# A decode kernel: wo kept in 36 KB rows by head and quarter of d, O placed there by a masked copy, and 36 transposes of h in place of 144

## The chip, the cores and the metric

The kernel runs on one core of one Trainium2 chip. The metric is device time in microseconds (us); the runs of one kernel in one set lie within 0.12% of each other. "Mix" is the last VectorE instruction, which adds the two gated branches; the output stores follow it. Engine names are those of the profile: PE is TensorE, PEld its weight loads, DVE VectorE, ACT ScalarE, POOL GpSimd, SP the queue that issues nearly all DMAs (556.93 of 557.24 MB in before). Times "at 1292.8 us" count from the start of the profiled span.

## The reference

For 8 sequences and one query token, D = 576, H = 32 heads, Sk = 4096 cached positions, Dh = 128, everything in bf16:

```python
q = (x @ wq).reshape(B, 1, H, Dh).transpose(0, 2, 1, 3)
p = softmax(einsum("bhqd,bhkd->bhqk", q, k_cache) * Dh ** -0.5)
a = einsum("bhqk,bhkd->bhqd", p, v_cache).transpose(...).reshape(B, 1, H * Dh) @ wo
b = gelu(layernorm(x) @ w1 + b1) @ w2 + b2            # F = 4608
g = sigmoid((x * gate_w).sum(-1))
return g * a + (1 - g) * b
```

The two caches are 537 MB of the 557 MB that are read.

## The kernel before

Three SBUF slots of 64 KB per partition hold all that streams: first wq, w1, w2, then the K and V tiles (8.4 MB each) of 32 groups of one sequence and 8 heads, then wo. The head of the program computes Q and the MLP. Its hidden rows h are transposed in 144 small matmuls:

```python
for c in range(4):
    for j in range(NJ):                                   # NJ = 36
        o = ht_ps[c][32 * c:32 * c + 32, j * B:(j + 1) * B]
        i = hrow[32 * c:32 * c + B, j::NJ]
        p_hT = op("tensor", lambda e, ...: e.matmul(o, lhsT=i, rhs=ident[32*c:32*c+B, 32*c:32*c+B], ...), ...)
    v_hT.append(op("vector", ... copy of that quarter to hT_sb ...))
```

Groups 0 and 1 are unrolled; groups 2 to 31 are ten turns of a loop of three. Each group multiplies K by q on DVE, sums on PE, takes the softmax, and does P times V on PE (PV), which ACT takes out of PSUM (`evict`). `gather` then adds the diagonal blocks with a selection matmul and `norm` divides. Every third group PE turns three O rows (`turn`, 16 matmuls), DVE takes the result out of PSUM (`stage`), and POOL puts it into OT (`place_o`):

```python
for r in range(WR):                                       # WR = 4
    i = Orow[:, r::WR]
    for h4 in range(4):
        p_tp[k] = op("tensor", ... e.matmul(tp_ps[32*h4:32*h4+32, r*8:(r+1)*8], lhsT=i, rhs=ident[...], ...), ...)
```

In the tail, wo arrives in five loads with 4.6 and 2.3 KB in a row, and three quarters of the output projection is issued before the turn of the last two groups:

```python
WO = ((0, 4, 0, 4), (4, 6, 0, 4), (6, 7, 0, 4), (7, 8, 0, 2), (7, 8, 2, 4))
...
pv(last); evict(last); gather(last); norm(last)
a_proj(range(6), ...)                 # 96 of 128 matmuls: heads of earlier groups
turn(last // GL, False); stage(last // GL); place_o(last // GL)
p_a = a_proj(range(6, WM), ...)       # 32 matmuls
```

Of the kernel before, what the change touches and what calls it, by code (L numbers as in the profile page):

```python
# [37 lines left out]
WM = H // 4  # L38
G0 = 2
GL = 3  # L40
WR = 4
# [149 lines left out]
def bass_gated_mix__mha_block_cached__mixer_channel_mlp__decode_kernel(  # L191
# [40 lines left out]
    wo_sb = view(SL, WO_SLOT * SLOT, [128, WM, WR * D])  # L232
# [41 lines left out]
    ones = sb("ones", [128, 1], F32)  # L274
    acc = sb("acc", [128, GL, HB], F32)
    OTs = sb("OTs", [128, 2, WR, 4], BF16)
# [3 lines left out]
    Orow = sb("Orow", [128, DH], BF16)  # L280
    OT = sb("OT", [128, WM, WR, B], BF16)
# [19 lines left out]
    bank = [nc.alloc_psum_tensor(f"psb{i}", [128, 512], F32) for i in range(8)]  # L301
# [4 lines left out]
    tp_ps = bank[6]  # L306
    y_ps = bank[7]
    up_ps = [bank[4], bank[5], bank[6]]
    ht_ps = bank[0:4]
# [77 lines left out]
    c_Or = memset("gpsimd", Orow[:], 0.0)  # L387

    def own_head(t, inside, outside):

        a = memset("gpsimd", t[:], inside)
        a = op("gpsimd", lambda e: e.affine_select(out=t[:], in_=t[:], compare_op=ALU.is_ge, fill=outside, base=0,
                                                   pattern=[[-PH, HB]], channel_multiplier=1), [a])
        return op("gpsimd", lambda e: e.affine_select(out=t[:], in_=t[:], compare_op=ALU.is_ge, fill=outside,
                                                      base=PH - 1, pattern=[[PH, HB]], channel_multiplier=-1), [a])

    c_ones = memset("gpsimd", ones[:], 1.0)
    c_hneg = own_head(hneg, 0.0, -60000.0)
    c_ps = [memset("vector", bank[i][:, :], 0.0) for i in (0, 1, 4, 5, 6)]
    c_yps = memset("vector", y_ps[:, :], 0.0)  # L400
# [3 lines left out]
        axis=AX.X, op=ALU.add), [c_id])  # L404
    c_Rows = op("vector", lambda e: e.tensor_reduce(
# [102 lines left out]
    v_hT = []  # L508
    for c in range(4):
        for j in range(NJ):  # L510
            o = ht_ps[c][32 * c:32 * c + 32, j * B:(j + 1) * B]
            i = hrow[32 * c:32 * c + B, j::NJ]
            p_hT = op("tensor", lambda e, o=o, i=i, c=c: e.matmul(  # L513
                o, lhsT=i, rhs=ident[32 * c:32 * c + B, 32 * c:32 * c + B], start=True, stop=True),
                [*v_hrow, *a_Q] if c == j == 0 else ())
        v_hT.append(op("vector", lambda e, c=c: e.tensor_copy(
            out=hT_sb[32 * c:32 * c + 32, :, :].rearrange("p j b -> p (j b)"),
            in_=ht_ps[c][32 * c:32 * c + 32, 0:NJ * B]), [p_hT]))
# [9 lines left out]
    for jt in range(NJ):  # L528
# [9 lines left out]
    a_qb, v_mult, v_red, p_sum, v_nm, a_exp, p_pv, a_ev, p_z, p_oz, v_norm, p_tp, v_st, g_ot, g_qm, p_q = (  # L538
        {} for _ in range(16))
    tp_of = bass.AP(tensor=tp_ps, offset=0, ap=[[pstride(tp_ps), 128], [4, 2], [8, WR], [1, 4]])  # L540

    def q_of(g):
# [5 lines left out]
            [*a_Q, c_sel32, a_ev[g - 3] if looped else p_q.get(g - 1)], token="tensor" if looped else None)  # L548
# [77 lines left out]
    def gather(g):  # L626
        looped = in_loop(g + 2)
        p_z[g] = op("tensor", lambda e: e.matmul(  # L628
            oz_ps[0:HB, DH:DH + 1], lhsT=acc[:, place(g), :], rhs=ones[:, :], start=True, stop=True),
            [a_ev[g], v_norm.get(g - 1), c_ones, *v_hb])  # L630
        for tt in range(TQ):
            p_oz[g] = op("tensor", lambda e, tt=tt: e.matmul(  # L632
                oz_ps[0:HB, 0:DH], lhsT=sel32[:, :, tt], rhs=O_sb[:, tt, :], start=(tt == 0), stop=(tt == TQ - 1)),
                [c_sel32] if tt == 0 else (), token="vector" if looped and tt == TQ - 1 else None)
# [60 lines left out]
    for g in range(NG):  # L695
# [4 lines left out]
        def between(c, g=g, k=k):  # L700
            if c == 1:
                q_of(g + 1)
            if in_loop(g) and place(g) == 0:
                if c == 2:
                    turn(k, True)
                if c == 4:
                    stage(k)
# [85 lines left out]
```

## Time and profile before

| | before |
|---|---|
| time, median of 3 runs | 1297.93 us (1297.68 to 1298.09) |
| span profiled | 1296.3 us |
| busy share PE / DVE / ACT / POOL | 56 / 62 / 12 / 3% |
| DMA, mean of 16 engines | 430 GB/s, 99.5% by the SP queue |
| last wo landing, mix | 1292.8 us, 1293.18 us |

The page of the kernel before: busy us by engine, then the DMA share and the GB/s in 40 slices of the span, then two of the DMA queues with packets, MB and share of 16 engines' span:

```profile
PE 731.7 (56%) x5202; PEld 339.4 (26%) x5202; DVE 804.7 (62%) x833; ACT 160.9 (12%) x587; POOL 40.7 (3%) x82
...
DMA  9999999999999999999999999999999999999997
GB/s 394 436 433 433 434 433 432 433 431 439 433 433 433 431 439 433 433 433 431 439 429 437 433 431 439 429 437 433 431 437 431 437 433 429 439 431 435 435 429 331
...
q1 hardware_dynamic: 11200, 556.93, 99.5%
q8 instruction: 10, 0.16, 0.1%
```

DMA is full from the first slice to the last but one. PE, DVE, ACT and POOL never bound the middle; only the last slice, at 331 GB/s, has something to give.

Two of the costliest groups of before (line, engine, operation, output<-inputs, shapes, count | busy us, mean ns | idle before, and what ended it):

```profile
L561 DVE TENSOR_TENSOR SL<-SL,q_bc 128x4096 bf16<-128x4096 bf16 x256 | 581.4, 2281 | 329.6 <-DMA SL<-in_A_k_cache_dram 329.6
...
L513 PE MATMUL psb<-ident,SL 8*32 8x8 bf16 x144 | 8.0, 196 | 6.6 <-DVE SL L504 6.6
```

DVE stands idle 329.6 us, about 10 us per group, for K to land. The 144 transposes cost PE 8.0 us.

The end of the chain of waits of before (start, us, what):

```profile
1268.56 24.22 DMA SL<-in_A_wo_dram
...
1292.83 0.33 PE psb L523 x8
...
1293.18 0.37 DVE out_sb L753
```

and what the engines did meanwhile, from its timeline:

```profile
1280.34 5.16 PE L617 MATMUL psb<-SL,P 128*32 128x512 bf16 x64 [2.81 <-DMA SL<-in_A_v_cache_dram]
...
1287.04 1.27 PE L523 MATMUL psb<-SL,OT 128*8 128x144 bf16 x58
...
1290.02 0.67 PE L523 MATMUL psb<-SL,OT 128*8 128x144 bf16 x32 [1.71 <-DMA SL<-in_A_wo_dram]
...
1291.13 0.34 POOL L662 COPY OT<-OTs 128x8 bf16<-128x8 bf16 x2 [19.27 <-DVE OTs L657]
...
1291.62 0.81 PE L523 MATMUL psb<-SL,OT 128*8 128x144 bf16 x24 [0.82 <-POOL OT L662]
```

The chain ends on the last wo load, with eight matmuls (0.33 us) behind it. The compute path (last V, PV, gather, turn, POOL's copy, 24 matmuls) is finished at 1291.62 + 0.81 = 1292.43 us, and then waits 0.4 us for wo. It had waited for wo before: the 32 matmuls at 1290.02 us, behind which the turn comes, stood 1.71 us for the second load.

The DMA view of before, of 1289 to 1292.5 us in 40 slices of 0.09 us, shows how the stream drains:

```profile
GB/s 316 448 290 342 290 369 237 290 316 316 211 290 184 211 132 158 105 132 79 79 26 26 53 53 240 26 26 26 26 26 26 26 26 26 26 26 26 26 0 0
```

433 GB/s, the rate of the middle slices, over 16 engines is 27 GB/s for one (an estimate). The run of 26 is one engine alone, finishing its wo rows for over a microsecond after the others are done (the single 240 is a 16 KB packet of queue 8, whose kind the page gives as "instruction"; such a packet is called a fetch below).

### The profile page before, as it was taken

To read this page: it belongs to the slowest core of one execution; us is meant where nothing else is said; L and a number is where in the kernel's file an instruction comes from. 1 tells how busy PE (TensorE), PEld (TensorE's weight loads), DVE (VectorE), ACT (ScalarE), POOL (GpSimd) and SP (SyncE) were. 2 spreads that over 40 slices of the span, in tenths; PEclk is the share of its full clock that TensorE was granted. 3 is DMA by queue.
4 is the path that set the end of the run, shared out by engine and by line. 5 is a ranking of instruction groups with operands and counts; after the bars stand their busy time and mean duration, and the time that the engine had idled before them with its cause. 6 is when DMAs were issued, how large, how long until landed. Compare 5 with 4: busy or idle time off the path is not lost.

```text
span 1296.3 us, 12332 instructions
## 1 busy us (share of the span) xinstructions
PE 731.7 (56%) x5202; PEld 339.4 (26%) x5202; DVE 804.7 (62%) x833; ACT 160.9 (12%) x587; POOL 40.7 (3%) x82
## 2 busy tenths in 40 slices
PE   3577566555566555556555556545556655546655
PEld 1423223122222222223222223222222222223213
DVE  2387667655567665567765567765567765566761
ACT  1011110111110011110011111011111011111011
POOL 1000000000000000000000000000000000000000
PEclk8588898787898778888877898887799878789878
DMA  9999999999999999999999999999999999999997
GB/s 394 436 433 433 434 433 432 433 431 439 433 433 433 431 439 433 433 433 431 439 429 437 433 431 439 429 437 433 431 437 431 437 433 429 439 431 435 435 429 331
DMA packets 11406, 557.24 MB, mean 430 GB/s; under 512 B 1360, under 2 KB 1376, under 8 KB 2816
## 3 DMA queue, kind: packets, MB, share of 16 engines
q1 hardware_dynamic: 11200, 556.93, 99.5%
q8 instruction: 10, 0.16, 0.1%
q10 hardware_dynamic: 192, 0.11, 0.0%
q14 instruction: 4, 0.03, 0.0%
HBM read 557.03 MB, written 0.01 MB: 430 GB/s over the span
## 4 chain that ended last, share of the span: by engine, by line
DMA 56%; DVE 25%; PE 13%; ACT 5%; issue 1%; SPq 0%; ACTq 0%
DMA SL<-in_A_k_cache_dram 53%; DVE SL L561 20%; PE psb L566 7%; DVE s_sb L572 5%; ACT P L606 4%; PE psb L617 4%; DMA SL<-in_A_wo_dram 2%; DMA SL<-in_A_wq_dram 1%; PE psb L632 1%; ACT O_sb L623 1%; PE psb L472 0%; SPq L317 0%; PE psb L628 0%; DVE OTs L657 0%; DVE mA L591 0%
## 5 line engine op out<-in xcount | busy, mean ns | idle before, releaser
L566 PE MATMUL psb<-SL,ident 128*128 128x512 bf16 x2048 | 550.1, 421 | 519.4 <-DVE SL L561 518.9
L561 DVE TENSOR_TENSOR SL<-SL,q_bc 128x4096 bf16<-128x4096 bf16 x256 | 581.4, 2281 | 329.6 <-DMA SL<-in_A_k_cache_dram 329.6
L566 PEld LDWEIGHTS psb<-SL,ident 128*128 128x128 bf16 x2048 | 199.7, 106 | 852.8 <-DVE SL L561 612.1
L572 DVE TENSOR_REDUCE s_sb<-psb 128x32 f32<-128x512 f32 x256 | 175.0, 684 | 91.0 <-PE psb L566 91.0
L606 ACT ACTIVATE P<-s_sb,hb 128x256 bf16<-128x256 f32 x256 | 126.3, 494 | 660.8 <-PE psb L617 643.9
L617 PE MATMUL psb<-SL,P 128*32 128x512 bf16 x2048 | 127.0, 386 | 2.8 <-DMA SL<-in_A_v_cache_dram 2.8
L617 PEld LDWEIGHTS psb<-SL,P 128*32 128x32 bf16 x2048 | 95.8, 153 | 20.4 <-DMA SL<-in_A_v_cache_dram 3.3
L545 POOL TENSOR_SCALAR Qm<-Q,sel 128x256 bf16<-128x256 bf16 x33 | 32.6, 987 | 1030.7 <-ACT O_sb L623 967.1
L553 ACT ACTIVATE q_bc<-psb 128x128 bf16<-128x128 f32 x33 | 9.1, 277 | 420.2 <-PE psb L550 420.2
L606 ACT ACTIVATION_READ_ACCUMULATOR P<-s_sb,hb 128x1 f32 x256 | 47.7, 186 | 0.0
L632 PE MATMUL psb<-O_sb,sel 128*8 128x128 f32 x256 | 33.9, 276 | 0.0
L632 PEld LDWEIGHTS psb<-O_sb,sel 128*8 128x8 f32 x256 | 21.8, 93 | 3.0
L623 ACT ACTIVATE O_sb<-psb 128x512 f32<-128x512 f32 x32 | 18.4, 574 | 10.0 <-PE psb L617 10.0
L638 DVE RECIPROCAL rz<-psb 8x1 f32<-8x1 f32 x32 | 4.8, 149 | 15.5 <-PE psb L632 15.5
L591 DVE TENSOR_REDUCE mA<-s_sb 128x1 f32<-128x256 f32 x32 | 13.4, 420 | 1.1
L494 DVE TENSOR_TENSOR SL<-psb,SL 104x384 f32<-104x384 f32 x3 | 1.7, 552 | 18.7 <-PE psb L490 18.7
L662 POOL COPY OT<-OTs 128x8 bf16<-128x8 bf16 x32 | 5.1, 218 | 219.1 <-DVE OTs L657 219.1
L640 DVE TENSOR_SCALAR Orow<-psb,rz 8x128 bf16<-8x128 f32 x32 | 10.9, 341 | 1.3 <-DVE rz L638 0.2
L513 PE MATMUL psb<-ident,SL 8*32 8x8 bf16 x144 | 8.0, 196 | 6.6 <-DVE SL L504 6.6
L490 PE MATMUL psb<-SL 128*8 128x384 bf16 x60 | 5.8, 519 | 7.1 <-DMA SL<-in_B_w_dram 7.1
L513 PEld LDWEIGHTS psb<-ident,SL 8*32 8x32 bf16 x144 | 7.9, 148 | 7.3 <-DVE SL L504 7.3
L628 PE MATMUL psb<-ones,acc 128*8 128x1 f32 x64 | 6.3, 167 | 5.3 <-ACT O_sb L623 5.3
(71 smaller groups left out, 111.6 us busy)
## 6 DMA issues: line engine op xcount, KB each, us to landing
SL<-in_B_w_dram SPq DMA_DIRECT2D x1, 5184.0 KB, 38.7
SL<-in_B_w_dram SPq DMA_DIRECT2D x1, 4608.0 KB, 25.0
SL<-in_A_wq_dram SPq DMA_DIRECT2D x1, 4096.0 KB, 13.6
SL<-in_A_wo_dram SPq DMA_DIRECT2D x1, 2304.0 KB, 19.4
SL<-in_A_wo_dram SPq DMA_DIRECT2D x1, 1152.0 KB, 23.0
SL<-in_B_w_dram SPq DMA_DIRECT2D x1, 576.0 KB, 26.0
SL<-in_A_wo_dram SPq DMA_DIRECT2D x1, 576.0 KB, 23.8
SL<-in_A_wo_dram SPq DMA_DIRECT2D x2, 288.0 KB, 24.1
```

The costliest lines, as they stand in the source:

```text
L513: p_hT = op("tensor", lambda e, o=o, i=i, c=c: e.matmul(o, lhsT=i, rhs=ident[32 * c:32 * c + B, 32 * c:32 * c + B], start=True, stop=True) ...
L545: g_qm[g] = op("gpsimd", lambda e: e.tensor_scalar(out=Qm[:, :, :].rearrange("p k d -> p (k d)"), in0=Q4[:, 2 * hg * DH:(2 * hg + 2) * DH] ...
L553: a_qb[g] = op("scalar", lambda e: e.activation(out=q_bc[:, place(g), :], in_=qb_ps[:, 0:DH], func=ACT.Copy), [p_q[g]], token="vector" if ...
L561: v_mult[g, c] = op("vector", lambda e: e.tensor_tensor(out=part, in0=part, in1=qb, op=ALU.mult), [land["k", g], a_qb[g]], token="tensor" ...
L566: p_sum[g, c] = op("tensor", lambda e, r=r, n=n: e.matmul(tr_ps[par][:, :], lhsT=ident[:, :], rhs=r, start=(n == 0), stop=(n == NCH - 1)), ...
L572: v_red[g, c] = op("vector", lambda e: e.tensor_reduce(out=s_sb[:, c * CT:(c + 1) * CT], in_=tr_ps[par][:, :].rearrange("p (t c) -> p t c" ...
L591: t = op("vector", lambda e: e.tensor_reduce(out=mA[:, 0:1], in_=s_sb[:, :], axis=AX.X, op=ALU.max), [v_red[g, NCK - 1], c_mA], token=own)
L606: a_exp[g] = op("scalar", lambda e, h=h: e.activation(out=P[:, h, :], in_=s_sb[:, :], func=ACT.Exp, bias=hb8[:, h:h + 1], scale=1.0, accum ...
L617: p_pv[g] = op("tensor", lambda e, o=o, tq=tq: e.matmul(o, lhsT=P[:, :, :].rearrange("p h t -> p (h t)")[:, tq::NTQ], rhs=vb[:, tq::NTQ, : ...
L623: a_ev[g] = op("scalar", lambda e: e.activation(out=O_sb[:].rearrange("p t d -> p (t d)"), in_=o_ps[:, :], func=ACT.Copy), [p_pv[g], p_z.g ...
L632: p_oz[g] = op("tensor", lambda e, tt=tt: e.matmul(oz_ps[0:HB, 0:DH], lhsT=sel32[:, :, tt], rhs=O_sb[:, tt, :], start=(tt == 0), stop=(tt ...
L640: v_norm[g] = op("vector", lambda e: e.tensor_scalar(out=Orow[32 * (g % GL):32 * (g % GL) + HB, :], in0=oz_ps[0:HB, 0:DH], scalar1=rz[0:HB ...
```

## The change

The intent: take work off PE. wo is laid out by 128 rows of 32 x 576 values, row p = (head, quarter of d), so each partition holds 36 KB contiguous in memory. O goes there without a turn: the gather repeats each head over four partitions (`selq`), DVE keeps on each the quarter that belongs to it (mask `dqm`) and folds, and POOL copies once per three groups into the 32 partitions of OT. The 144 transposes of h become 36 with all four quarters at once. PSUM becomes one tensor, cleared by one memset.

```diff
-    for c in range(4):
-        for j in range(NJ):
-            ... 144 matmuls, rhs = 8x8 identity
+    per_quarter = bass.AP(tensor=ident, offset=0, ap=[[pstride(ident), QP], [32, 4], [1, B]])
+    for j in range(NJ):
+        p_hT = op("tensor", lambda e, j=j: e.matmul(
+            ht_ps[0:32, j, :, :], lhsT=hrow[0:QP, j::NJ], rhs=per_quarter, start=True, stop=True), ...)
 ...
     def norm(g):
-        reciprocal; tensor_scalar -> Orow
+        t = tensor_reduce(zs <- oz_ps[0:32, DH:DH + HB]);  t = reciprocal(rz <- zs)
+        t = scalar_tensor_tensor(On <- oz_ps[0:32, 0:DH] * rz * dqm)
+        v_norm[g] = tensor_reduce(OTs[:, :, place(g + 2)] <- On by quarter)
-    def turn(k, looped): ... 16 matmuls
-    def stage(k): ...
+    def place_o(engine, g0, g1): ... OT[32 * hg:32 * hg + 32, :, b:b + n] <- OTs
 ...
-    WO = ((0, 4, 0, 4), (4, 6, 0, 4), (6, 7, 0, 4), (7, 8, 0, 2), (7, 8, 2, 4))
+    WO = ((0, 24), (24, 30), (30, 32))
 ...
-    a_proj(range(6), ...); turn(...); stage(...); place_o(...); p_a = a_proj(range(6, WM), ...)
+    place_o("vector", last - 1, last + 1)
+    for j in range(NJO):                                   # NJO = 32: all 128 matmuls after O
+        p_a = quarters(OT[:, j, :], wo_sb[:, j, :], j == 0, j == NJO - 1, [ld_wo[j], v_bx, *g_ot.values()])
```

More of the change, by code (lines that the diff above doesn't have):

```diff
@@ L37 @@
 FB = FC // 3
-WM = H // 4
+NDQ = 4
+NJO = H * DH // 128
 G0 = 2
 GL = 3
-WR = 4
 class Stream:
@@ L231, in bass_gated_mix__mha_block_cached__mixer_channel_mlp__decode_kernel @@
     WO_SLOT = (2 * NG + 3) % 3
-    wo_sb = view(SL, WO_SLOT * SLOT, [128, WM, WR * D])
+    wo_sb = view(SL, WO_SLOT * SLOT, [128, NJO, D])
     class Tail:
@@ L273, in bass_gated_mix__mha_block_cached__mixer_channel_mlp__decode_kernel @@
     Sel = sb("Sel", [128, 64], BF16)
-    ones = sb("ones", [128, 1], F32)
+    hsel = sb("hsel", [128, HB * NDQ], F32)
+    selq = sb("selq", [128, TQ, HB * NDQ], F32)
+    zs = sb("zs", [32, 1], F32)
     acc = sb("acc", [128, GL, HB], F32)
-    OTs = sb("OTs", [128, 2, WR, 4], BF16)
+    OTs = sb("OTs", [32, NJO, GL], F32)
+    On = sb("On", [32, DH], F32)
+    dqm = sb("dqm", [32, NDQ], F32)
     Rows = sb("Rows", [128, 4], F32)
@@ L279, in bass_gated_mix__mha_block_cached__mixer_channel_mlp__decode_kernel @@
     q_bc = sb("q_bc", [128, GL, DH], BF16)
-    Orow = sb("Orow", [128, DH], BF16)
-    OT = sb("OT", [128, WM, WR, B], BF16)
+    OT = sb("OT", [128, NJO, B], BF16)
     bmg_sb = sb("bmg_sb", [128, QN], F32)
@@ L298, in bass_gated_mix__mha_block_cached__mixer_channel_mlp__decode_kernel @@
     rz = sb("rz", [128, 1], F32)
-    bank = [nc.alloc_psum_tensor(f"psb{i}", [128, 512], F32) for i in range(8)]
+    PS = nc.alloc_psum_tensor("PS", [128, 8 * 512], F32)
+    bank = [PS[:, 512 * i:512 * (i + 1)] for i in range(8)]
     tr_ps = bank[0:2]
@@ L305, in bass_gated_mix__mha_block_cached__mixer_channel_mlp__decode_kernel @@
     oz_ps = bank[5]
-    tp_ps = bank[6]
     y_ps = bank[7]
     up_ps = [bank[4], bank[5], bank[6]]
-    ht_ps = bank[0:4]
+    ht_ps = PS[:, 0:NJ * 32].rearrange("p (j c b) -> p j c b", j=NJ, c=4)
     xt_ps = bank[7]
@@ L386, in bass_gated_mix__mha_block_cached__mixer_channel_mlp__decode_kernel @@
     c_mA = memset("gpsimd", mA[:], 0.0)
-    c_Or = memset("gpsimd", Orow[:], 0.0)
-    def own_head(t, inside, outside):
-        a = memset("gpsimd", t[:], inside)
-        a = op("gpsimd", lambda e: e.affine_select(out=t[:], in_=t[:], compare_op=ALU.is_ge, fill=outside, base=0,
-                                                   pattern=[[-PH, HB]], channel_multiplier=1), [a])
-        return op("gpsimd", lambda e: e.affine_select(out=t[:], in_=t[:], compare_op=ALU.is_ge, fill=outside,
-                                                      base=PH - 1, pattern=[[PH, HB]], channel_multiplier=-1), [a])
-    c_ones = memset("gpsimd", ones[:], 1.0)
-    c_hneg = own_head(hneg, 0.0, -60000.0)
-    c_ps = [memset("vector", bank[i][:, :], 0.0) for i in (0, 1, 4, 5, 6)]
-    c_yps = memset("vector", y_ps[:, :], 0.0)
+    c_ones = memset("gpsimd", hsel[:], 1.0)
+    per_head = hsel[:].rearrange("p (h q) -> p h q", q=NDQ)
+    t = op("gpsimd", lambda e: e.affine_select(out=per_head, in_=per_head, compare_op=ALU.is_ge, fill=0.0, base=0,
+                                               pattern=[[-PH, HB], [0, NDQ]], channel_multiplier=1), [c_ones])
+    c_hsel = op("gpsimd", lambda e: e.affine_select(out=per_head, in_=per_head, compare_op=ALU.is_ge, fill=0.0,
+                                                    base=PH - 1, pattern=[[PH, HB], [0, NDQ]], channel_multiplier=-1), [t])
+    c_hneg = op("vector", lambda e: e.tensor_scalar(out=hneg[:, :], in0=hsel[:, ::NDQ], scalar1=-1.0, scalar2=60000.0,
+                                                    op0=ALU.add, op1=ALU.mult), [c_hsel])
+    c_yps = memset("vector", PS[:, :], 0.0)
+    c_ps = [c_yps]
+    c_dqm = op("vector", lambda e: e.tensor_reduce(
+        out=dqm[:], in_=bass.AP(tensor=ident, offset=0, ap=[[pstride(ident), 32], [1, NDQ], [NDQ, 8]]),
+        axis=AX.X, op=ALU.add), [c_id])
     c_sel32 = op("vector", lambda e: e.tensor_reduce(
@@ L404, in bass_gated_mix__mha_block_cached__mixer_channel_mlp__decode_kernel @@
         axis=AX.X, op=ALU.add), [c_id])
+    c_selq = op("vector", lambda e: e.tensor_copy(
+        out=selq[:].rearrange("p t (h q) -> p t h q", q=NDQ),
+        in_=bass.AP(tensor=sel32, offset=0, ap=[[pstride(sel32), 128], [1, TQ], [TQ, HB], [0, NDQ]])), [c_sel32])
     c_Rows = op("vector", lambda e: e.tensor_reduce(
@@ L506, in bass_gated_mix__mha_block_cached__mixer_channel_mlp__decode_kernel @@
     free[1] = [p_up]
-    v_hT = []
-    for c in range(4):
-        for j in range(NJ):
-            o = ht_ps[c][32 * c:32 * c + 32, j * B:(j + 1) * B]
-            i = hrow[32 * c:32 * c + B, j::NJ]
-            p_hT = op("tensor", lambda e, o=o, i=i, c=c: e.matmul(
-                o, lhsT=i, rhs=ident[32 * c:32 * c + B, 32 * c:32 * c + B], start=True, stop=True),
-                [*v_hrow, *a_Q] if c == j == 0 else ())
-        v_hT.append(op("vector", lambda e, c=c: e.tensor_copy(
-            out=hT_sb[32 * c:32 * c + 32, :, :].rearrange("p j b -> p (j b)"),
-            in_=ht_ps[c][32 * c:32 * c + 32, 0:NJ * B]), [p_hT]))
+    per_quarter = bass.AP(tensor=ident, offset=0, ap=[[pstride(ident), QP], [32, 4], [1, B]])
+    for j in range(NJ):
+        p_hT = op("tensor", lambda e, j=j: e.matmul(
+            ht_ps[0:32, j, :, :], lhsT=hrow[0:QP, j::NJ], rhs=per_quarter, start=True, stop=True),
+            [*v_hrow, *a_Q] if j == 0 else ())
+    v_hT = [op("vector", lambda e, c=c: e.tensor_copy(
+        out=hT_sb[32 * c:32 * c + 32, :, :], in_=ht_ps[0:32, :, c, :]), [p_hT]) for c in range(4)]
     def quarters(lhsT, w, first, stop, waits):
@@ L535, in bass_gated_mix__mha_block_cached__mixer_channel_mlp__decode_kernel @@
     free[2] = [p_down]
-    a_qb, v_mult, v_red, p_sum, v_nm, a_exp, p_pv, a_ev, p_z, p_oz, v_norm, p_tp, v_st, g_ot, g_qm, p_q = (
-        {} for _ in range(16))
-    tp_of = bass.AP(tensor=tp_ps, offset=0, ap=[[pstride(tp_ps), 128], [4, 2], [8, WR], [1, 4]])
+    a_qb, v_mult, v_red, p_sum, v_nm, a_exp, p_pv, a_ev, p_z, p_oz, v_norm, g_ot, g_qm, p_q = ({} for _ in range(14))
     def q_of(g):
@@ L547, in q_of @@
             scalar1=sel32[:, b // TQ, b % TQ:b % TQ + 1], scalar2=None, op0=ALU.mult),
-            [*a_Q, c_sel32, a_ev[g - 3] if looped else p_q.get(g - 1)], token="tensor" if looped else None)
+            [*a_Q, c_sel32, a_ev[g - 3] if looped else p_q.get(g - 1), *list(g_ot.values())[-1:]], token="tensor" if looped else None)
         for k in range(2):
@@ L628, in gather @@
         p_z[g] = op("tensor", lambda e: e.matmul(
-            oz_ps[0:HB, DH:DH + 1], lhsT=acc[:, place(g), :], rhs=ones[:, :], start=True, stop=True),
-            [a_ev[g], v_norm.get(g - 1), c_ones, *v_hb])
+            oz_ps[0:32, DH:DH + HB], lhsT=hsel[:, :], rhs=acc[:, place(g), :], start=True, stop=True),
+            [a_ev[g], v_norm.get(g - 1), c_hsel, *v_hb])
         for tt in range(TQ):
             p_oz[g] = op("tensor", lambda e, tt=tt: e.matmul(
-                oz_ps[0:HB, 0:DH], lhsT=sel32[:, :, tt], rhs=O_sb[:, tt, :], start=(tt == 0), stop=(tt == TQ - 1)),
-                [c_sel32] if tt == 0 else (), token="vector" if looped and tt == TQ - 1 else None)
+                oz_ps[0:32, 0:DH], lhsT=selq[:, tt, :], rhs=O_sb[:, tt, :], start=(tt == 0),
+                stop=(tt == TQ - 1)), [c_selq] if tt == 0 else (),
+                token="vector" if looped and tt == TQ - 1 else None)
@@ L636, in norm @@
     def norm(g):
-        looped = in_loop(g + 2)
-        t = op("vector", lambda e: e.reciprocal(out=rz[0:HB, :], in_=oz_ps[0:HB, DH:DH + 1]), [p_oz[g]],
-               token="vector" if looped else None)
-        v_norm[g] = op("vector", lambda e: e.tensor_scalar(
-            out=Orow[32 * (g % GL):32 * (g % GL) + HB, :], in0=oz_ps[0:HB, 0:DH], scalar1=rz[0:HB, 0:1], scalar2=None,
-            op0=ALU.mult), [t, c_Or, p_tp.get(g // GL - 1) if not looped else None])
-    def turn(k, looped):
-        for r in range(WR):
-            i = Orow[:, r::WR]
-            for h4 in range(4):
-                p_tp[k] = op("tensor", lambda e, r=r, h4=h4, i=i: e.matmul(
-                    tp_ps[32 * h4:32 * h4 + 32, r * 8:(r + 1) * 8], lhsT=i,
-                    rhs=bass.AP(tensor=ident, offset=h4, ap=[[pstride(ident), 128], [4, 2], [32, 4]]),
-                    start=True, stop=True),
-                    [v_norm.get(min(GL * k + GL, NG) - 1), v_st.get(k - 1), *v_hb] if r == h4 == 0 else (),
-                    token="vector" if looped and r == WR - 1 and h4 == 3 else None)
@@ L656, in stage @@
-    def stage(k):
-        v_st[k] = op("vector", lambda e: e.tensor_copy(out=OTs[:, :, :, :], in_=tp_of), [p_tp[k], g_ot.get(k - 1)])
-    def place_o(k):
-        for g in range(GL * k, min(GL * k + GL, NG)):
+        own = "vector" if in_loop(g + 2) else None
+        t = op("vector", lambda e: e.tensor_reduce(out=zs[:, :], in_=oz_ps[0:32, DH:DH + HB], axis=AX.X, op=ALU.add),
+               [p_oz[g]], token=own)
+        t = op("vector", lambda e: e.reciprocal(out=rz[0:32, :], in_=zs[:, :]), [t], token=own)
@@ new lines, in norm @@
+        t = op("vector", lambda e: e.scalar_tensor_tensor(
+            out=On[:, :].rearrange("p (q j) -> p q j", q=NDQ), in0=oz_ps[0:32, 0:DH].rearrange("p (q j) -> p q j", q=NDQ),
+            scalar=rz[0:32, 0:1], in1=bass.AP(tensor=dqm, offset=0, ap=[[pstride(dqm), 32], [1, NDQ], [0, NJO]]),
+            op0=ALU.mult, op1=ALU.mult), [t, c_dqm], token=own)
+        v_norm[g] = op("vector", lambda e: e.tensor_reduce(
+            out=OTs[:, :, place(g + 2)], in_=On[:, :].rearrange("p (q j) -> p j q", q=NDQ), axis=AX.X, op=ALU.add),
+            [t, *list(g_ot.values())[-1:]])
@@ L661, in place_o @@
+    def place_o(engine, g0, g1):
+        g, t = g0, None
+        while g < g1:
             hg, b = divmod(g, B)
-            g_ot[k] = op("gpsimd", lambda e, hg=hg, b=b, g=g: e.tensor_copy(
-                out=OT[:, 2 * hg:2 * hg + 2, :, b], in_=OTs[:, :, :, g % GL]), [v_st[k]])
+            n = min(g1 - g, B - b)
+            t = g_ot[g0] = op(engine, lambda e, hg=hg, b=b, n=n, at=g - g0: e.tensor_copy(
+                out=OT[32 * hg:32 * hg + 32, :, b:b + n], in_=OTs[:, :, at:at + n]), [v_norm[g1 - 1], t])
+            g += n
@@ L681, in bass_gated_mix__mha_block_cached__mixer_channel_mlp__decode_kernel @@
     next_load()
-    WO = ((0, 4, 0, 4), (4, 6, 0, 4), (6, 7, 0, 4), (7, 8, 0, 2), (7, 8, 2, 4))
+    WO = ((0, 24), (24, 30), (30, 32))
     ld_wo = {}
     def load_wo(waits):
-        for n, (m0, m1, r0, r1) in enumerate(WO):
-            src = bass.AP(tensor=A_wo.tensor, offset=A_wo.offset + m0 * 512 * D + r0 * D,
-                          ap=[[WR * D, 128], [512 * D, m1 - m0], [1, (r1 - r0) * D]])
-            t = load("sync", wo_sb[:, m0:m1, r0 * D:r1 * D], src, f"ld_wo{n}", waits)
-            for m in range(m0, m1):
-                for r in range(r0, r1):
-                    ld_wo[m, r] = t
+        w = A_wo.rearrange("(p j) n -> p j n", j=NJO)
+        for n, (j0, j1) in enumerate(WO):
+            t = load("sync", wo_sb[:, j0:j1, :], w[:, j0:j1, :], f"ld_wo{n}", waits)
+            ld_wo.update({j: t for j in range(j0, j1)})
     for g in range(NG):
@@ L697, in bass_gated_mix__mha_block_cached__mixer_channel_mlp__decode_kernel, with between @@
             S.mark()
-        k = (g - G0) // GL - 1
-        def between(c, g=g, k=k):
+        def between(c, g=g):
             if c == 1:
                 q_of(g + 1)
-            if in_loop(g) and place(g) == 0:
-                if c == 2:
-                    turn(k, True)
-                if c == 4:
-                    stage(k)
         scores(g, between)
         if in_loop(g):
-            if place(g) == 0 and k >= 0:
-                place_o(k)
             gather(g - 2)
@@ L723, in bass_gated_mix__mha_block_cached__mixer_channel_mlp__decode_kernel @@
             norm(g - 2)
+            if place(g) == GL - 1:
+                place_o("gpsimd", g - GL - 1, g - 1)
         exps(g)
@@ L730, in bass_gated_mix__mha_block_cached__mixer_channel_mlp__decode_kernel @@
     last = NG - 1
-    turn(last // GL - 1, False)
-    stage(last // GL - 1)
-    place_o(last // GL - 1)
     gather(last - 1)
@@ L739, in bass_gated_mix__mha_block_cached__mixer_channel_mlp__decode_kernel @@
     norm(last)
-    def a_proj(ms, turned):
-        for m in ms:
-            for r in range(WR):
-                at = quarters(OT[:, m, r, :], wo_sb[:, m, r * D:(r + 1) * D], m == r == 0, m == WM - 1 and r == WR - 1,
-                              [ld_wo[m, r], v_bx, *turned])
-        return at
-    a_proj(range(6), list(g_ot.values()))
-    turn(last // GL, False)
-    stage(last // GL)
-    place_o(last // GL)
-    p_a = a_proj(range(6, WM), list(g_ot.values()))
+    place_o("vector", last - 1, last + 1)
+    for j in range(NJO):
+        p_a = quarters(OT[:, j, :], wo_sb[:, j, :], j == 0, j == NJO - 1,
+                       [ld_wo[j], v_bx, *g_ot.values()])
     t = op("vector", lambda e: e.scalar_tensor_tensor(
```

## The prediction

> **What bounds the kernel now.** The DMA stream. In the 40 slices the DMA row is at 9 tenths or more in 39, at a mean of 430 GB/s over 557 MB; queue 1 alone fills 99.5% of 16 engines' span. [...] PE (56%), DVE (62%), ACT (12%), POOL (3%) are under it: DVE idles 329.6 us for K loads (costliest groups). The queue is never empty: K loads take 43.4 us, V loads 33.1 us from issue to landing, where one needs 19.5 us.
>
> **What changes, and what lies on the path.**
> 1. Head. The 144 transposes of h (8.0 us, their copies mostly hidden; timeline, 40.6 to 49.2 us) become 36, an estimated 2 us, then four copies of 0.46 us: w2's slot comes free 4 to 5 us before 55.3 us. V's load into it is issued sooner, but queues behind two K loads, the first landing only at 60.8 us. Gain: 0. One memset of all 8 PSUM banks (6 took 3.19 us, so about 4.3), now behind a POOL mask, delays the LayerNorm chain about 4 us, into the wait for wq (PE idles 4.0 us before 15.99 us); Q may slip a few tenths. K's load is issued at 21 us into a queue full until 39 us. Cost: 0.
> 2. Loop. 16 turns per three groups leave PE; DVE gets four small instructions (estimated 0.9 us) for two (0.49 us), per group of 39 us. All in idle time. Cost: 0.
> 3. Tail, the only place where compute matters. Now the last wo chunk lands at 1292.8 us (chain of waits: 24.2 us of DMA), then 8 matmuls (0.33 us), mix (0.37 us), stores, to 1296.3 us. PE's last turn, POOL's copy (1290.5 to 1291.6 us) and 24 matmuls end at 1292.4 us, 0.4 us before the DMA: the removed turn is almost, not quite, on the path. The wo packets grow from 4.6 and 2.3 KB (1152) to 27.6, 6.9 and 2.3 KB (384). While wo streamed, 1280 to 1288 us, the rate was 407 to 412 GB/s instead of 433: 5% of 11 us, so its end should come 0.5 us sooner. The drain is ragged: from 1289.5 to 1292.5 us DMA share falls from 0.74 to 0.05, a few engines finishing late; larger packets may shorten it. New: O is ready at about 1288.7 us, but 96 of 128 matmuls wait for one load of three quarters of wo, due about 1289.7 us; 128 at 21 ns are 2.7 us, so PE ends about 1292.4 us, together with the last load. Gain: 0.5 us.
>
> **Prediction.** 1297.4 us, 8 in 10 within 1296.2 to 1298.6. Chance of faster by over 2%: 0.005; within 2%: 0.99; slower: 0.005.
>
> **What would show it.** Right: middle slices unchanged at 430 to 433 GB/s; the first K landing at 60.8 us; bmg done 4 to 5 us earlier with nothing later moving; a chain of waits ending wo DMA, few matmuls, mix; the mix at 1292.6 us instead of 1293.2. Wrong: another rate in the loop; a later first K; PE last in the chain by more than 1 us.
>
> **What would make it wrong.** A TensorE clock of 0.5 (as at 1273 to 1283 us) during the last 128 matmuls, 2.5 us; POOL copies or a late q delaying DVE beyond its 10 us of slack; the ragged drain coming from wo's small packets, 1 to 2 us more gain.

The sum is 0 for the head, 0 for the loop and 0.5 us for the tail, so 1297.4 us from the 1297.93 us of before. Estimates from the trace of before are the 19.5 us for one load (8.4 MB at 430 GB/s), the 21 ns for a matmul (32 in 0.67 us) and the 0.5 us itself (5% of 11 us), which supposes that larger packets bring back the whole of the lower rate.

## The result, and the profile after

The changed kernel takes 1296.80 us (median of 6, 1296.61 to 1297.22) against 1297.85 us (median of 6, 1297.65 to 1298.09) of before: 1.05 us less. Ratios are the mean time of one kernel's fast runs over that of the other's of the same rounds, so not quite the ratio of these medians; here 0.9993 with a 95% interval of 0.998 to 1.0005. By that interval the kernels are the same; but all six runs of the changed kernel lie under all six of before, and a second set on another chip gives 1297.00 (1296.71 to 1297.23, 5 runs) against 1297.91 us. About one microsecond, 0.08%, is there.

The page after:

```profile
PE 720.0 (56%) x4902; PEld 333.8 (26%) x4902; DVE 821.5 (63%) x884; ACT 160.9 (12%) x587; POOL 41.0 (3%) x60
...
GB/s 395 437 428 440 430 436 430 433 435 433 433 431 435 437 429 433 433 435 437 425 437 435 433 431 431 437 435 431 435 429 437 435 427 435 435 435 431 429 439 343
...
q1 hardware_dynamic: 10400, 556.93, 99.5%
q8 instruction: 9, 0.15, 0.0%
```

PE lost 11.7 us of work and 300 matmuls, DVE gained 16.8 us, and the slices between the first and the last move the same GB/s, slice by slice within a few per cent. The SP queue moves the same bytes in 800 fewer packets; queue 8 has 9 packets instead of 10.

The end of the chain of waits after:

```profile
1236.94 43.38 DMA SL<-in_A_v_cache_dram
...
1280.36 6.04 PE PS L617 x34
...
1286.43 0.61 ACT O_sb L623
...
1287.31 0.91 PE PS L632 x8
...
1289.38 0.20 DVE OT L656
...
1289.72 2.20 PE PS L525 x128
...
1291.94 0.37 DVE out_sb L727
```

The chain has changed its kind. It no longer ends on wo but runs through compute from the last V landing: PV, eviction, gather, norm, all 128 projection matmuls without a wait. The mix is 1.24 us sooner; the last V load is not (first PV matmul at 1280.36 us, before 1280.34). The last wo load lands 23.8 us after its issue at 1267.5 us, at 1291.3 us instead of 1292.8.

The drain after, in the same window of the DMA view:

```profile
GB/s 184 342 158 237 316 184 290 316 211 211 211 132 53 79 79 79 53 26 26 26 26 0 0 0 0 0 0 0 0 0 0 0 0 0 0 0 187 0 0 0
```

The lone engine at 26 GB/s is left for four slices, 0.35 us, where before it was there for well over one microsecond.

So two questions: what brought wo's landing 1.5 us forward (the prediction had 0.5), and what is the removed turn worth?

### The profile page after: what moved, and what is told of

It reads as the page before. It is cut to its first block, busy times and chain, and to the rows that moved or that the text cites. A ratio compares the mean times of both kernels' runs of the same rounds, so it can differ in the third digit from the quotient of the medians.

```text
span 1295.0 us, 11764 instructions
## 1 busy us (share of the span) xinstructions
PE 720.0 (56%) x4902; PEld 333.8 (26%) x4902; DVE 821.5 (63%) x884; ACT 160.9 (12%) x587; POOL 41.0 (3%) x60
## 4 chain that ended last, share of the span: by engine, by line
DMA 57%; DVE 23%; PE 13%; ACT 5%; issue 1%; ACTq 0%; SPq 0%
DMA SL<-in_A_k_cache_dram 53%; DVE SL L561 19%; PE PS L566 7%; PE PS L617 5%; ACT P L606 4%; DVE s_sb L572 4%; DMA SL<-in_A_v_cache_dram 3%; DMA SL<-in_A_wq_dram 1%; PE PS L632 1%; ACT O_sb L623 1%; PE PS L478 0%; PE PS L628 0%; PE PS L525 0%; SPq L320 0%; DVE OTs L646 0%
## 5 line engine op out<-in xcount | busy, mean ns | idle before, releaser
L566 PE MATMUL PS<-SL,ident 128*128 128x512 bf16 x2048 | 546.9, 419 | 530.3 <-DVE SL L561 530.3
L566 PEld LDWEIGHTS PS<-SL,ident 128*128 128x128 bf16 x2048 | 198.9, 106 | 865.3 <-DVE SL L561 627.4
L572 DVE TENSOR_REDUCE s_sb<-PS 128x32 f32<-128x512 f32 x256 | 175.1, 684 | 89.9 <-PE PS L566 89.7
L617 PE MATMUL PS<-SL,P 128*32 128x512 bf16 x2048 | 127.9, 387 | 2.7 <-DMA SL<-in_A_v_cache_dram 2.7
L617 PEld LDWEIGHTS PS<-SL,P 128*32 128x32 bf16 x2048 | 95.8, 152 | 21.1 <-DMA SL<-in_A_v_cache_dram 3.1
L632 PE MATMUL PS<-O_sb,selq 128*32 128x128 f32 x256 | 34.1, 278 | 0.0
L632 PEld LDWEIGHTS PS<-O_sb,selq 128*32 128x32 f32 x256 | 26.1, 113 | 0.2
L623 ACT ACTIVATE O_sb<-PS 128x512 f32<-128x512 f32 x32 | 18.4, 575 | 10.8 <-PE PS L617 10.8
L646 DVE TENSOR_REDUCE OTs<-On 32x32 f32<-32x128 f32 x32 | 11.9, 371 | 1.1
L642 DVE SCALAR_TENSOR_TENSOR On<-PS,rz,dqm 32x128 f32<-32x128 f32 x32 | 10.8, 339 | 1.2
L500 DVE TENSOR_TENSOR SL<-PS,SL 104x384 f32<-104x384 f32 x3 | 1.7, 552 | 15.3 <-PE PS L496 15.3
```

Source lines behind the costliest of these rows:

```text
L566: p_sum[g, c] = op("tensor", lambda e, r=r, n=n: e.matmul(tr_ps[par][:, :], lhsT=ident[:, :], rhs=r, start=(n == 0), stop=(n == NCH - 1)), ...
L572: v_red[g, c] = op("vector", lambda e: e.tensor_reduce(out=s_sb[:, c * CT:(c + 1) * CT], in_=tr_ps[par][:, :].rearrange("p (t c) -> p t c" ...
L617: p_pv[g] = op("tensor", lambda e, o=o, tq=tq: e.matmul(o, lhsT=P[:, :, :].rearrange("p h t -> p (h t)")[:, tq::NTQ], rhs=vb[:, tq::NTQ, : ...
L623: a_ev[g] = op("scalar", lambda e: e.activation(out=O_sb[:].rearrange("p t d -> p (t d)"), in_=o_ps[:, :], func=ACT.Copy), [p_pv[g], p_z.g ...
L632: p_oz[g] = op("tensor", lambda e, tt=tt: e.matmul(oz_ps[0:32, 0:DH], lhsT=selq[:, tt, :], rhs=O_sb[:, tt, :], start=(tt == 0), stop=(tt = ...
L642: t = op("vector", lambda e: e.scalar_tensor_tensor(out=On[:, :].rearrange("p (q j) -> p q j", q=NDQ), in0=oz_ps[0:32, 0:DH].rearrange("p ...
```

## The experiments

Twelve kernels; names with b are made from the kernel before, with a from the changed one. The interval of every ratio is about plus or minus 0.0014, or 1.8 us. So medians and their ranges, on one chip, are read together with what the trace shows, and differences of 0.2 us are not argued from. The kernel before took 1297.76 us (1297.60 to 1298.38), 1297.64 (1297.46 to 1297.86) and 1297.91 (1297.45 to 1298.31), 9 runs each.

| run | median us (range of 5) | ratio to before | last wo landing, us | mix, us |
|---|---|---|---|---|
| b_wo75 | 1296.59 (1296.24 to 1296.79) | 0.9989 | cut | 1292.05 |
| a_wo75 | 1296.86 (1295.91 to 1297.06) | 0.9990 | cut | 1292.58 |
| a_small | 1297.24 (1296.88 to 1297.92) | 0.9996 | 1291.6 | 1292.04 |
| b_wo3 | 1298.03 (1297.62 to 1299.06) | 1.0000 | 1292.4 | 1294.08 |
| b_h36 | 1297.15 (1297.05 to 1297.34) | 0.9996 | 1291.8 | 1292.18 |
| a_norm3 | 1296.59 (1296.56 to 1297.11) | 0.9993 | 1291.4 | 1291.82 |
| a_vh | 1298.17 (1297.56 to 1298.73) | 1.0004 | 1291.9 | 1293.22 |
| b_vh | 1298.24 (1297.84 to 1298.51) | 1.0004 | 1293.3 | 1293.79 |
| b_h36_pad | 1297.77 (1297.74 to 1298.21) | 1.0000 | 1292.4 | 1292.77 |
| a_pad | 1296.96 (1296.60 to 1297.58) | 0.9994 | 1291.3 | 1292.14 |
| a_ztail | 1297.70 (1296.71 to 1298.05) | 0.9996 | 1291.4 | 1291.83 |
| a_again | 1297.00 (1296.71 to 1297.23) | 0.9993 | 1291.4 | 1292.41 |

Landings are the last issue plus its time to landing. The mix is that of the one profiled run, so it is not always the median run (b_wo3's was its slowest). The profile of before (landing 1292.8, mix 1293.18 us) is of a run of 1298.07 us, 0.1 to 0.4 us above its medians, so differences of landing or mix to it are on the large side.

### What ended the kernel before, and what ends it now: b_wo75 and a_wo75

```diff
 # b_wo75: the last three of five loads left out
-    WO = ((0, 4, 0, 4), (4, 6, 0, 4), (6, 7, 0, 4), (7, 8, 0, 2), (7, 8, 2, 4))
+    WO = ((0, 4, 0, 4), (4, 6, 0, 4))
 # a_wo75: the last two of three loads left out
-    WO = ((0, 24), (24, 30), (30, 32))
+    WO = ((0, 24),)
```

Both leave out the last quarter of wo's bytes and compute a wrong result. (The comparison with the reference evidently does not resolve this part of the output.)

> The kernel before without its last three wo loads (25% of wo; wrong result on purpose, the matmuls read what the K slot held). Theory: before ended on the last wo landing (1292.8 us); without it the turn of the last two groups and POOL's copy end last, mix at about 1292.45 us instead of 1293.18: 0.7 us faster, about 1297.1 us. Rival (before was already limited by its compute path): no change, 1297.85 us.

> The changed kernel without its last two wo loads (25% of wo; wrong result on purpose). Theory: the changed kernel ends on compute after the last V landing, so no change: 1296.8 us, mix still at about 1291.9 us. Rival (it still ends on wo): faster by 0.3 us or more. The difference of this run to the same cut of before is what the removed turn is worth by itself: theory 0.3 to 0.6 us.

Without the last quarter, before is faster by 1.17 us, all five runs below all nine of before on that chip. That is more than the 0.7 us expected: the turn came sooner too (the last 32 matmuls began at 1291.32 us, where the last 32 of before began at 1291.62), as the second wo load, for which it waits, landed 0.2 us sooner. The changed kernel does not move (1296.86 against 1296.80 and 1297.00 elsewhere). So before ended on wo and the changed kernel does not; that much is shown. The ends of their chains of waits, b_wo75 first:

```profile
1291.14 0.13 POOL OT L662
...
1291.32 0.70 PE psb L523 x32
...
1292.05 0.37 DVE out_sb L753
```

```profile
1290.02 0.20 DVE OT L656
...
1290.36 2.20 PE PS L525 x128
...
1292.58 0.37 DVE out_sb L727
```

Their difference is what the new compute path is worth by itself, with wo out of the way. I expected 0.3 to 0.6 us for the changed kernel; the runs give 0.27 us to before, which is to say nothing measurable. In before the turn and POOL's copy come after 96 of the 128 matmuls, and only 32 (0.70 us) follow O. In the changed kernel O needs no turn, but all 128 (2.20 us) follow it. From the start of PV (1280.41 and 1280.43 us) to the mix it is 11.64 us in the one and 12.15 in the other, of which 0.35 us is a longer PV in a_wo75 (6.59 against 6.24 us, at a granted clock of 0.65 from 1280 to 1289 us where b_wo75 has 0.69). The removed turn gained nothing here. (In b_wo75 PE still waited 0.37 us for the second wo load ahead of its turn; without that, the old order would, if anything, have come out better.)

### How much of wo's earlier landing is the packets: a_small and b_wo3

```diff
 # a_small: same three loads, 64 bytes of gap after every 4 rows (2 rows from j = 24)
-    wo_sb = view(SL, WO_SLOT * SLOT, [128, NJO, D])
+    P4, P2 = 4 * D + 32, 2 * D + 32
+    wo_4 = view(SL, WO_SLOT * SLOT, [128, 6, P4])
+    wo_2 = view(SL, WO_SLOT * SLOT + 6 * P4, [128, 4, P2])
 # b_wo3: before with three loads
-    WO = ((0, 4, 0, 4), (4, 6, 0, 4), (6, 7, 0, 4), (7, 8, 0, 2), (7, 8, 2, 4))
+    WO = ((0, 6, 0, 4), (6, 7, 0, 4), (7, 8, 0, 4))
```

> The changed kernel with the same three wo loads, but cut into packets of 4.6 and 2.3 KB by a gap of 64 bytes in the destination. Theory (the small packets were only 0.45 us of the 1.5 us by which wo landed sooner; the rest was one engine held up by an instruction fetch): the last wo landing moves from 1291.3 to about 1291.75 us, mix at 1292.0 to 1292.1 us, 1296.8 to 1297.0 us. Rival (the packets are all of it): last landing at about 1292.8 us, mix at 1293.1 us, 1297.9 us.

> The kernel before with its wo in three loads (75%, 12.5%, 12.5% of the bytes, nearly the same packets) instead of five, the fifth of which kept the queue's issue busy for 9 us. Theory (the number of loads does not matter): last landing near 1292.6 us, 1297.7 to 1297.9 us. Rival (five loads and the blocked issue delayed the last landing): landing at about 1291.6 us, then limited by the turn: 1297.1 us.

With small packets the changed kernel's chain of waits ends on wo again, barely:

```profile
1267.65 24.00 DMA SL<-in_A_wo_dram
...
1291.69 0.33 PE PS L527 x8
...
1292.04 0.37 DVE out_sb L733
```

wo lands at 1291.6 us, 0.3 us later than with large packets and 1.1 us earlier than before. The packet records in the trace give the same size from below: in before a 4608-byte packet came every 179 ns on an engine and a 2304-byte one every 90 ns, so an engine's 56 and 16 of them are 11.46 us; after, 8 each of 27.6, 6.9 and 2.3 KB, at 1026, 261 and 90 ns, are 11.02 us. For the largest of each that is 25.7 against 26.9 GB/s on one engine. The packets are 0.3 to 0.45 us of 1.5. The median is 0.44 us above the changed kernel's, on another chip and in ranges that overlap; the rival's 1297.9 was reached by one run of five.

The number of loads is no cause: b_wo3 lands at 1292.4 us and is at 1298.03 us, if anything slower, because three quarters in one load (landed at 1289.6 us) pushes 96 matmuls and the turn behind them later.

### What the rest is: b_h36

```diff
 # the 36 transposes of h alone, in the kernel before (with PSUM as one tensor)
-    for c in range(4): for j in range(NJ): ... 144 matmuls
+    for j in range(NJ): ... 36 matmuls, then the four copies
```

> The kernel before with the 36 transposes of h alone. Theory: V's first load is issued about 5 us sooner but lands when it did, the first K multiply starts at 60.5 to 60.8 us, no change: 1297.85 us. Rival (the head's time counts): up to 5 us faster.

My theory fell. I had put this part's worth at exactly zero, and it gave 0.49 us, all five runs below all nine of before. The rival, that the head's time counts, is not borne out by the trace either. The V load into w2's slot, and the first K multiply, in before:

```profile
55.33 0.33 SPq L374 DMA_DIRECT2D SL<-in_A_v_cache_dram  x1
...
60.78 4.49 DVE L561 TENSOR_TENSOR SL<-SL,q_bc 128x4096 bf16<-128x4096 bf16 x2 [4.58 <-DMA SL<-in_A_k_cache_dram]
```

and in b_h36:

```profile
48.76 0.33 SPq L375 DMA_DIRECT2D SL<-in_A_v_cache_dram  x1
...
60.44 4.49 DVE L558 TENSOR_TENSOR SL<-SL,q_bc 128x4096 bf16<-128x4096 bf16 x2 [10.89 <-DMA SL<-in_A_k_cache_dram]
```

The 6.6 us by which V is issued sooner became 0.34 us, and none of it arrived at the last V load (first PV matmul at 1280.45 us, 0.1 later than before). But wo landed 1.0 us sooner, and the drain shows the lone engine left for four slices, as in the changed kernel. Drain of b_h36:

```profile
GB/s 316 421 342 263 421 263 316 263 316 237 290 237 237 263 237 372 184 132 105 79 79 53 26 26 26 26 0 0 0 0 0 0 0 0 0 0 0 0 0 0
```

What else differs is queue 8. Every packet of it has 16384 bytes in the trace (0.16 MB in 10). b_h36 has 9 of these fetches, before 10. Taken out are 108 transposes with a weight load each, so 216 instructions of PE. That a fetch brings instructions for PE, and that fewer instructions need fewer fetches, I supposed from the name of the kind and from these counts; no trace shows it.

A fetch is not free where DMA is the bound. In before such a packet took 1.1 us (at 1286 us), in which the wo packets in flight fell from 16.3 to 15.3, and the two after it took 494 and 335 ns where the rest take 178 to 188. Together that is 1.5 to 1.6 us of one DMA engine (an estimate: 1.1 us, and what the two packets took beyond 182 ns each). The drain of before shows one engine working on alone at 26 GB/s, and PE waited for it: of the 16 semaphore records of the last wo load the last came at 1292.78 us, the one before it 1.09 us earlier, and the eight matmuls began at 1292.83 us. So what delays one engine can delay the landing.

New theory: fewer PE instructions spare a fetch, a DMA engine that comes last is relieved of it, and wo lands sooner.

### Instructions put back, without the work: b_h36_pad and a_pad

```diff
+    for _ in range(108):                      # after the MLP; PE is idle there
+        op("tensor", lambda e: e.matmul(PS[0:32, 3 * 512:3 * 512 + 8], lhsT=ident[:, 0:32],
+                                        rhs=ident[:, 0:8], start=True, stop=True))
```

> The kernel before with the 36 transposes of h, and 108 small matmuls into an unused bank after the MLP, so that PE has as many instructions as before. New theory (the fewer PE instructions spare one 16 KB instruction fetch, which holds one DMA engine for 1.1 us; this is why the 36 transposes alone gave 0.5 us): 10 fetches again, last wo landing back at about 1292.6 us, about 1297.7 us. Rival (the sooner end of the head is what counts): as the 36 transposes alone, 9 fetches or not, 1297.15 us.

> The changed kernel with the same 108 small matmuls added. New theory: 10 fetches instead of 9, last wo landing from 1291.2 to about 1292.2 us, which then ends the kernel: mix at about 1292.5 us instead of 1291.9, 1297.3 us. Rival (large packets and the removed turn are the whole gain): 1296.8 us.

b_h36_pad is back at 1297.77 us, within the range of before on its chip (0.14 us under its median), where the 36 transposes without the padding were 0.49 us under theirs. Its V load is still issued at 49.4 us, so that the sooner V load is intact; PE is busy with the padding until 54.9 us, but the first K multiply waits for DMA here as in b_h36. The fetch is back (its page counts 10), and so is a long drain, in the same window with two engines and then one:

```profile
GB/s 369 369 342 316 290 263 263 290 290 263 290 263 237 263 211 184 105 105 105 105 105 53 53 53 53 53 53 53 53 26 26 26 26 0 0 0 187 0 0 0
```

That the instruction count, and not the sooner V load, made b_h36 faster is shown by this pair, within the scatter of the runs on two chips. That it did so by sparing a fetch is not: the tenth fetch of b_h36_pad begins at 1292.15 us, when its last wo packet has ended (1291.96). Up to there it had 9, like b_h36.

a_pad is a miss: 1296.96 us, the same as a_again (1297.00). It has 9 fetches, not the 10 that I had counted on: one more before 1280 us than the changed kernel, but none between 1280 us and 1290.8, where the changed kernel has one at 1288. So as many come before wo's last bytes as without the padding, and wo lands at 1291.3 us as without it. The count of instructions alone thus does not decide what is fetched when.

What the trace settles: no view of `prof` tells the DMA engines apart, but the semaphore records in the traces do. They hold, for every load, the 16 times at which its count rose by one; I take them as one for each of the 16 engines. Here they are, in order and in us from their median, for the wo loads before and after the fetch (labels: landing of the load), read from trace.npz:

```text
before 1286.03: -1.35 -0.88 -0.85 -0.61 -0.38 -0.30 -0.02 -0.00 0.00 0.11 0.16 0.44 0.51 0.64 0.66 1.11
before 1289.97: -1.34 -0.89 -0.83 -0.61 -0.39 -0.30 -0.02 -0.01 0.01 0.10 0.14 0.41 0.50 0.62 1.10 2.20
b_h36  1286.12: -1.44 -1.27 -0.90 -0.89 -0.79 -0.71 -0.20 -0.02 0.02 0.06 0.19 0.28 0.39 0.64 0.76 1.05
b_h36  1288.98: -1.48 -0.93 -0.92 -0.81 -0.72 -0.29 -0.05 -0.01 0.01 0.16 0.17 0.27 0.37 0.64 0.69 1.04
```

The lags last while the queue is full: in before the last one is 1.08 us behind the median at 235 us and 1.11 at 1280 us. Across the fetch one number moves by about 1.5 us, the loss that the packet records gave, while the other fifteen keep their places within 0.06 us. In before, 0.66 becomes 2.20: the engine that fetched is the one that then drains alone. In b_h36 the fetch (at 1284.1 us) took an engine that was 1.27 us ahead; it falls to 0.17 behind, and the last engine is as late as it was.

All the profiles fit. In twelve of them the fetch put one engine back by 1.4 to 1.6 us. In the five kernels with 144 transposes or their padding (before, b_wo75, b_wo3, b_vh, b_h36_pad) the fetch took an engine 0.1 to 0.7 us behind the median, which so became the last, 1.6 to 2.2 behind. In seven with 36 (b_h36, the changed kernel twice, a_norm3, a_small, a_ztail, a_vh) it took one 1.3 to 1.7 us ahead, and the last engine stayed 0.9 to 1.1 behind. In a_wo75 no number moves by more than 0.13 (its first engines were through with their only wo load when the fetch began), and a_pad has no fetch until its wo is through: it lost nothing by its padding.

So the new theory was half right. In these profiles an engine held up by a fetch came last unless it was 1.3 us or more ahead, but what b_h36 gained is not a fetch fewer: in it, in before and in b_h36_pad alike a fetch falls into the wo loads, and which engine it took went with the instruction count. How that engine is chosen, and so whether another count would do as well, stays open.

The same records part the landing of wo in two. The mean of the 16 times of the last load is 1290.59 to 1290.70 us with small packets (before, b_wo3, b_h36_pad, b_h36, a_small) and 1290.20 to 1290.35 with large ones (the changed kernel twice, a_norm3, a_ztail, a_pad): the packets, 0.2 to 0.5 us. The last engine comes 1.67 to 2.11 us after that mean in before, b_wo3 and b_h36_pad, and 0.99 to 1.23 in the other seven: the fetch, 0.4 to 1.1 us.

### Whether the new DVE work costs: a_norm3

```diff
             norm(g - 2)
+            norm(g - 2)
+            norm(g - 2)
```

> The changed kernel with the four norm instructions run three times in the loop (same result): about 60 us more DVE work. Theory: it fits in DVE's 10 us of idle time per group, no change: 1296.8 us. Rival (the added DVE work of the change takes back part of its gain): each norm costs a part of its 1.0 us per group, so 5 to 60 us slower.

```profile
PE 721.5 (56%) x4902; PEld 332.9 (26%) x4902; DVE 876.7 (68%) x1124; ACT 160.9 (12%) x587; POOL 40.7 (3%) x60
```

DVE does 55 us more and the time is 1296.59 us, no slower. The loop's DVE work is free in the amount the change adds, and three times over.

### Less compute in the tail: a_vh, b_vh and a_ztail

If the changed kernel ends on compute behind the last V, shortening that should help until wo ends it. First, the last V in two halves:

```diff
+        if kind == "v" and g == NG - 1:
+            for i in range(2):                 # by position, each half with its own semaphore
+                ... land["v", g, i] = op("sync", ... dma_start of 32 of every 64 positions ...)
 ...
+            if g == NG - 1:                    # PV waits for one half at tq == 0, the other at tq == 32
```

> The changed kernel with the last V load in two halves with a semaphore each, so that half of the last PV matmuls run before the second half lands. Theory (the changed kernel ends on compute behind the last V landing): O is ready about 3 us sooner, and the last wo landing (1291.3 us) ends it again: mix at about 1291.6 us, 0.3 us faster, 1296.5 us. Rival: no change, 1296.8 us.

> The kernel before with the last V load in two halves. Theory: before ends on the last wo landing, so no more than 0.1 us: 1297.8 us. Rival (before was limited by compute behind V): 0.7 us faster or more, 1297.1 us.

Both became slower, by 0.5 and 0.6 us against before, and a_vh by about 1.5 against the changed kernel. The mechanism worked: in a_vh O is ready at 1286.2 us, three microseconds sooner. But then PE waits for the first wo load, and the end of the chain of waits is:

```profile
1266.52 22.59 DMA SL<-in_A_wo_dram
...
1289.16 4.04 PE PS L533 x128
...
1293.22 0.37 DVE out_sb L742
```

128 matmuls take 4.04 us where the changed kernel's take 2.20. The windows of a_vh (us, busy by engine, granted clock, DMA share, GB/s):

```profile
1285.00:1289.00 4.00, 0.00 (x0) 0.00 (x0) 1.08 (x5) 0.00 (x0) 0.00 (x0) 0.89 0.89 374
1289.00:1294.00 5.00, 4.01 (x128) 3.70 (x128) 0.37 (x1) 0.00 (x0) 0.00 (x0) 0.50 0.28 112
```

PE stood idle for 4.30 us before the 128 matmuls, and from 1289 to 1294 us the granted clock was 0.50. In the changed kernel they came after 1.51 us of idle time, at a granted clock of 1.00. I read from this that the wait which the earlier O brought cost PE its clock in the matmuls that mattered; no run varies the idle time alone. My expectation had no term for that.

Nor had it one for the DMA side. The halves go in packets of 8 KB where the whole V has 64 KB (b_vh has 12112 packets on queue 1, before 11200), and by the semaphore records the mean of the 16 times of the last V load is 0.67 us later in both kernels. So wo's last load lands 0.5 to 0.6 us later too: at 1291.9 us in a_vh, which at a granted clock of 1.00 could not have had its mix before 1292.3 us (an estimate: that landing and eight matmuls of 0.33 us), and at 1293.3 us in b_vh, whose chain ends on 32 matmuls that took 1.21 us at a granted clock of 0.50 (0.70 us at 1.00 in b_wo75).

Second, the last group's sum of exponentials and its reciprocal before PV instead of after it:

```diff
+    p_z[last] = matmul(bank[6][0:32, 0:HB], lhsT=hsel, rhs=acc[:, place(last), :])      # before pv(last)
+    zs, rz = tensor_reduce, reciprocal of it
     pv(last); evict(last); gather(last); norm(last)      # norm(last) without its first two instructions
```

> The changed kernel with the last group's sum of exponentials and its reciprocal done before the last PV instead of after it (another bank). Theory (the changed kernel ends on compute behind the last V landing, with wo's last landing 0.3 us behind): 0.6 us less chain, of which 0.3 to 0.4 us is left before wo's landing ends it: mix at about 1291.6 us, 1296.4 us. Rival: 1296.8 us.

The profiled run ends as expected, on wo, though with less to show for it than hoped:

```profile
1267.21 24.22 DMA SL<-in_A_wo_dram
...
1291.47 0.33 PE PS L525 x8
...
1291.83 0.37 DVE out_sb L737
```

Its span is 1294.9 us, the shorter one (a_again: 1295.5), but its time is 1297.70 us against 1297.00. Time minus span is 2.8 us in its profiled run where in those of all the others it is 1.6 to 1.9. In the others the last fetch comes before the span's end, in a_ztail's records one begins after it. This cannot be the whole cause: the two slowest of its five runs (1298.05 and 1297.88 us) have a difference of 1.7 to 1.8 us like the others, and spans of 1296.3 and 1296.2 us where the other three have 1294.9 to 1295.1. They were not profiled, so what slowed them stays open.

> The changed kernel as it is, on the same chip as the three above. Both theories: 1296.6 to 1296.9 us, 9 fetches, mix at about 1291.9 us.

The control held: 1297.00 us with 9 fetches, the chain ending on compute. Its mix is 0.5 us later than in the first profile (PV took 6.40 us; the granted clock was 0.87 from 1285 to 1289 us, in the first profile 0.98). Nothing tried beats the changed kernel beyond the scatter.

## Why the prediction was right or wrong

**The time and the class.** 1297.4 us was predicted, 1296.80 was measured, inside 1296.2 to 1298.6. The gain was 1.05 us where about 0.5 was forecast, and about half of it came by way of a cause that I had not named; that the time still fell inside is owed in part to the width of the range, which is luck. Same within 2% was right, and so was its reason: the stream of caches bounds the kernel, the slices in the middle move 425 to 440 GB/s before and after, and 11.7 us less PE work did not enter.

**Head, "Gain: 0".** This step failed. The head alone gave 0.49 us of the 1.05 (b_h36). The path that I followed, slot free sooner and V issued sooner, is indeed worth nothing: V is issued 6.6 us sooner and the last V lands no sooner. What I left out is that fetches take time of the DMA engines that carry wo (the packets in flight fell from 16.3 to 15.3 for 1.1 us), and that with another number of PE instructions a fetch held up another of these engines. Putting 108 empty matmuls back took most of the gain away (0.14 us under before instead of 0.49).

**Head, "bmg done 4 to 5 us earlier with nothing later moving".** Nearly: its instruction began 6.2 us earlier (49.18 against 55.34 us), and the first K multiply 0.3 us earlier.

**Head, "Cost: 0".** Right. The memset took 3.47 us, begun at 5.04 us, and the Q matmuls even began earlier (15.64 against 15.99 us).

**Loop, "Cost: 0".** Right; a_norm3 adds 55 us of DVE work without a loss.

**Tail, packets: "0.5 us sooner".** Right mechanism, nearly right size: 0.45 us by the packets' own cadence, 0.3 us in the landing, 0.2 to 0.5 in the mean over the engines, about 0.4 in the median.

**Tail, the ragged drain.** The prediction left open whether it came from wo's small packets. It did not: a_small keeps small packets and lands at 1291.6 us. Of the 1.5 us by which wo lands sooner, about 1.0 is there with the 36 transposes alone. The long drain of before was the engine that the fetch at 1285.8 us held up.

**Tail, "PE ends about 1292.4 us, together with the last load".** Off by half a microsecond: wo at 1291.3, PE at 1291.9. So the chain ends on compute and not, as predicted, on wo, matmuls and mix. The 128 matmuls took 2.20 us where 21 ns each had made 2.7, and O came 0.9 us later than the estimated 1288.7 (1289.6), mostly because PV took 6.0 us where the profile of before had 5.2; the granted clock from 1281 to 1285 us was 0.50, in before 0.70. That is not the change: with the PV of before, b_wo75 took 6.24 us.

**The turn, "almost, not quite, on the path".** True of before. I did not see that its removal would bring nothing: with wo out of the way the changed tail is no faster (1296.86 against 1296.59 us), since it gave up the 96 matmuls that before hid ahead of its turn.

**The clock.** Named as a danger, absent from the last 128 matmuls of the changed kernel (granted clock 1.00), and met in a_vh at its full size: 4.04 instead of 2.20 us, at 0.50.

So the microsecond is 0.5 us of fewer instructions (by way of the engine that a fetch took), 0.3 to 0.45 us of larger packets, and the rest within the scatter; it stops where the compute behind the last V takes over.

## What to carry to other kernels

Here the DMA stream was full from end to end, and 11.7 us less work on PE and 16.8 us more on DVE showed only in what happened around the last landing: 1.05 us in all. In such a kernel find that landing, see whether one DMA engine drains alone (26 GB/s for over a microsecond in before), and whether a fetch held that engine up. A gain of this kind may not outlast the next change of the instruction count: 108 matmuls more took b_h36 from 0.49 to 0.14 us under before (on another chip), and how the engine is chosen the runs do not show. A shorter compute path in the tail can lose: in a_vh O came three microseconds sooner, PE then idled 4.30 us, the last matmuls ran at a granted clock of 0.50, and the kernel was about 1.5 us slower than the changed one. And before taking a step out of a chain, ask what was hidden behind it: the 96 projection matmuls that ran ahead of the turn now stand after O.
